# Loading and converting the first layer's weights in units of one m instead of one k

## The chip, the cores and the metric

The kernel runs on one core of one Trainium2 chip. The metric is the device time of one execution in microseconds; a smaller number is better. Over three runs the kernel before has a median of 731.37 us (729.12 to 733.59).

## The reference, cut to what matters

```python
def reference(**kw):
    y = rwkv(r, k, v, w, u)            # (4, 8, 768, 48): a state per head, decayed by w per token
    x = y.transpose(0, 2, 1, 3).reshape(3072, 384)
    h = np.maximum(x @ w_in, 0.0)      # w_in  (384, 2048)
    x = h * h @ w_out                  # w_out (2048, 384)
    h = x @ w2_in                      # w2_in (384, 1024)
    sm = softmax(h)
    ln = layer_norm(h * sm) * g_ln
    return ln @ w2_out                 # w2_out (1024, 384)
```

All four weight matrices arrive as 8-byte floats, the rest as 4-byte floats. "First layer" below is the pair w_in and w_out.

## The kernel before, in words

Three stages follow one another on TensorE (PE): attention, first layer, second layer. Tokens go in 24 chunks of 128 (chunk c); four chunks make a block n of 512 tokens, and there are 6 blocks. Chunks 0 to 3 are block 0; the attention of chunks 4 to 7 (block 1) is interleaved with the first layer of block 0, and so on.

The first layer takes w_in's 2048 columns in 16 groups m of 128. A step is one (block, m); block 0's m = 0 to 3 are split in two steps of 256 tokens each, because chunks 0 and 1 are ready before 2 and 3. Each step has two parts. **P1** (`p1`, L650 to L659) is nine matmuls: for each k of 3, high x by high w_in, low x by high w_in, high x by low w_in. ScalarE (ACT) then applies relu and square and makes the high part `gh` (L656 to L658), and VectorE (DVE) the low part `gl` (L659). **P2** (`p2`, L669 to L673) is nine matmuls of gh and gl with w_out's 128 rows of this m, added up over m in three PSUM banks. P1 runs up to three steps ahead of P2.

Weights come as 8-byte floats and are turned into two 4-byte parts, high and low. A load puts one unit into one of six staging buffers `stg` (SyncE, SP, issues all loads in order). `w1_conv` converts a unit: DVE makes a 4-byte float in three operations (L591, L594, L597, with PSUM bank 2 as scratch), ACT casts the high part (L609, `wih` or `woh`), GpSimd (POOL) subtracts for the low part (L610, `wil` or `wol`), and the next load is issued for the freed buffer. A unit of w_in before is (k, g): 128 rows by 512 columns (512 KB), so that the four m of group g need three units. A unit of w_out is one m: 128 rows by 384 columns (384 KB).

What decides a chunk's x: its scores on PE (L424, later L437), a masked copy on DVE (L473, later L481, "the mask"), the product with v on PE (L540, later L514), and the split into `xh` on ACT (L570) and `xl` on DVE (L571). From chunk 4 on, ACT copies L514's result to `ys` and eight small DMAs (L524, L526) bring it to `xr` before the split. Chunk 7 is the last that block 1's first P1 needs.

A scheduler places the instructions of each engine when the kernel is built, by its own estimates; from then on every engine, and SP with its DMAs, runs strictly in that order. It starts from the order of the code, where `side[i]` is the list of extra work (conversions, attention) put ahead of step i.

Of the kernel before, what the change touches and what calls it, by code (L numbers as in the profile page):

```python
# [18 lines left out]
DM = H * D  # L19
KD = DM // 128  # L20
# [13 lines left out]
M1 = FF1 // 128  # L34
# [3 lines left out]
NST = 6  # L38
# [139 lines left out]
def rwkv_moe_moe2_kernel(ctx, tc, rkd, tok, tk2, wd, w, u, w_in, w_out, w2_in, w2_out, g_ln, out):  # L178
    nc = tc.nc
# [5 lines left out]
    ps = psp.tile([128, 8, 512], F32, name="ps")  # L185
# [62 lines left out]
            )  # L248

    def setup_masks():  # L250
        make_identity(nc, ident)
        nc.gpsimd.memset(mask, 1.0)
        nc.gpsimd.affine_select(
            out=mask, in_=mask, pattern=[[1, C]], compare_op=ALU.is_gt, fill=0.0, base=0, channel_multiplier=-1
        )
        nc.gpsimd.memset(epst[:, 0:1], -0.5)
# [345 lines left out]
    def split(st, hi, lo, scale=None):  # L602

        x = as_f32(st, ps[:, 2, :].bitcast(U32))
        if scale is not None:
            nc.gpsimd.tensor_tensor(out=x, in0=x, in1=scale.to_broadcast(list(x.shape)), op=ALU.mult)

        def finish():
            nc.scalar.copy(hi, x)  # L609
            nc.gpsimd.tensor_tensor(out=lo, in0=x, in1=hi.bitcast(F32), op=ALU.subtract)  # L610

        return finish

    W1 = []
    for g in range(4):
        W1 += [(0, (k, g)) for k in range(KD)] + [(1, 4 * g + q) for q in range(4)]
    w_ld, w_st = [0], []

    def w1_load(n=1):
        for _ in range(n):  # L620
            if w_ld[0] < len(W1):
                kind, g = W1[w_ld[0]]
                w_st.append((kind, g, load_unit((w_in, w_out)[kind], kind, g, nc.sync)))
                w_ld[0] += 1

    def w1_conv():
        kind, g, st = w_st.pop(0)
        weight_tiles(kind, g // 4 if kind else g[1])
        if kind:
            split(st, woh[g // 4][:, g % 4], wol[g // 4][:, g % 4])()  # L630
        else:
            split(st, wih[g[1]][:, g[0]], wil[g[1]][:, g[0]])()
        w1_load()

    steps = []
# [244 lines left out]

    nsteps = len(steps)
    side = {i: [] for i in range(first_full)}
    first_m = {m: i for i, (n, m, c0, sz) in reversed(list(enumerate(steps))) if n == 0}
    for g in range(4):
        for q, n in enumerate((2, 2, 3) if g < 3 else (1, 1, 1, 1)):
            side[first_m[4 * g + q]] += [w1_conv] * n
    for c in range(4):
        side[c].append(lambda c=c: (first_state(c), load_chunk(4 + c) if c < 2 else None))
    for q, c in enumerate(range(4, 8)):
# [151 lines left out]
```

## Time and profile before

| | us |
|---|---|
| median of three runs | 731.37 |
| the profiled execution | 732.05 |
| its span | 730.3 |
| PE busy in the span | 702.9 (96%) |
| DVE busy | 418.7 (57%) |
| ACT busy | 321.7 (44%) |
| POOL busy | 267.9 (37%) |

The profile comes from one execution, and its span is what the trace covers; 1.75 us of that execution lie outside it. A busy share is an average over the whole span. The first 130 us, in which attention and weights arrive, look quite unlike the rest, so they have to be read by stretches. The timeline gives, for each engine, the start and duration of an instruction, and in brackets how long the engine had been idle before it and what ended the wait.

### The profile page before, as it was taken

Reading aid. Unit: us, or ns where it says so; the run is one execution under the profiler, and the core shown is the slowest. Engines: PE = TensorE matmul, PEld = TensorE weight load, DVE = VectorE, ACT = ScalarE, POOL = GpSimd, SP = SyncE. Lnnn points to the kernel's source line nnn. Section 1 sums busy time; section 2 is a strip of 40 time slices with the busy share of each in tenths; the row PEclk is TensorE's granted clock in tenths of the full one; section 3 lists DMA queues with packets and bytes.
Section 4 is the critical chain, followed back from the end, with each engine's and each line's share of the span. In section 5 each row is a group of like instructions: output and inputs, shape, how many; then the busy total and the mean of one; then the engine's idle time right before and its main releaser. Section 6 shows DMA issues by size and latency. Waiting matters only on the chain.

```text
span 730.3 us, 13143 instructions
## 1 busy us (share of the span) xinstructions
PE 702.9 (96%) x5088; PEld 599.7 (82%) x5088; DVE 418.7 (57%) x752; ACT 321.7 (44%) x625; POOL 267.9 (37%) x297
## 2 busy tenths in 40 slices
PE   3799999999999999999999999999999999999996
PEld 3588768788888888888888888888899999999996
DVE  7799986444534334433333266614768767777671
ACT  1444645454554554555454455634433232322232
POOL 6969777444533333334222022802303030300000
PEclk9999999999999999999999999999999999999999
DMA  8956552222312222321161016221111100000001
GB/s 277 267 200 212 140 179 79 89 67 85 106 57 89 67 66 66 108 65 60 41 202 35 12 41 202 88 86 34 66 65 49 40 22 11 22 22 22 22 34 38
DMA packets 35113, 62.73 MB, mean 86 GB/s; under 512 B 7777, under 2 KB 17378, under 8 KB 35042
## 3 DMA queue, kind: packets, MB, share of 16 engines
q1 hardware_dynamic: 35042, 61.80, 27.2%
q8 instruction: 42, 0.69, 0.4%
q14 instruction: 29, 0.24, 0.1%
HBM read 48.41 MB, written 9.44 MB: 79 GB/s over the span
## 4 chain that ended last, share of the span: by engine, by line
PE 86%; DMA 7%; SPq 2%; POOL 2%; ACT 1%; issue 1%; DVE 0%; ACTq 0%; POOLq 0%; DVEq 0%
PE ps L651 9%; PE ps L653 8%; PE ps L652 8%; PE ps L670 8%; PE ps L669 8%; PE ps L673 8%; PE ps L819 5%; PE ps L818 5%; PE ps L821 5%; PE ps L755 5%; PE ps L757 5%; PE ps L756 5%; DMA stg<-in_w_out_dram 3%; PE ps L802 3%; PE ps L514 2%; PE ps L437 2%
## 5 line engine op out<-in xcount | busy, mean ns | idle before, releaser
L659 DVE TENSOR_TENSOR gl<-ps,gh 128x512 fp32r<-128x512 f32 (+1 forms) x100 | 66.7, 668 | 168.2 <-ACT gh L658 166.9
L651 PE MATMUL ps<-xh,wih 128*128 128x512 f32 (+1 forms) x300 | 117.5, 393 | 1.8 <-ACT xh L570 1.0
L653 PE MATMUL ps<-xh,wil 128*128 128x512 f32 (+1 forms) x300 | 115.2, 385 | 2.3 <-POOL wil L610 2.3
L669 PE MATMUL ps<-gh,woh 128*128 128x512 f32 (+1 forms) x300 | 113.3, 383 | 2.2 <-ACT gh L658 2.1
L652 PE MATMUL ps<-xl,wih 128*128 128x512 f32 (+1 forms) x300 | 115.0, 384 | 0.1
L670 PE MATMUL ps<-gh,wol 128*128 128x512 f32 (+1 forms) x300 | 113.3, 383 | 0.0
L656 ACT ACTIVATE ps<-ps 128x512 f32<-128x512 f32 (+1 forms) x100 | 56.3, 564 | 115.9 <-PE ps L653 115.4
L356 POOL TENSOR_TENSOR mv<-mv,pt 48x512 f32<-48x512 f32 x40 | 52.1, 1302 | 93.0 <-DMA mv<-in_rkd_dram 92.3
L673 PE MATMUL ps<-gl,woh 128*128 128x512 f32 (+1 forms) x300 | 83.3, 382 | 0.0
L653 PEld LDWEIGHTS ps<-xh,wil 128*128 128x128 f32 x300 | 56.7, 189 | 14.3 <-POOL wil L610 3.1
L651 PEld LDWEIGHTS ps<-xh,wih 128*128 128x128 f32 x300 | 56.4, 189 | 14.5 <-ACT xh L570 1.6
L669 PEld LDWEIGHTS ps<-gh,woh 128*128 128x128 f32 x300 | 56.0, 189 | 13.9 <-ACT gh L658 2.9
L652 PEld LDWEIGHTS ps<-xl,wih 128*128 128x128 f32 x300 | 56.8, 190 | 10.8 <-DVE xl L571 0.6
L818 PE MATMUL ps<-w2oh,lth 128*128 128x384 f32 x192 | 65.1, 339 | 0.2 <-ACT lth L811 0.2
L670 PEld LDWEIGHTS ps<-gh,wol 128*128 128x128 f32 x300 | 56.1, 189 | 11.2 <-issue 0.4
L819 PE MATMUL ps<-w2ol,lth 128*128 128x384 f32 x192 | 65.2, 339 | 0.0
L673 PEld LDWEIGHTS ps<-gl,woh 128*128 128x128 f32 x300 | 55.7, 189 | 10.9
L658 ACT CAST gh<-ps 128x512 fp32r<-128x512 f32 (+1 forms) x100 | 56.9, 571 | 2.8
L657 ACT ACTIVATE ps<-ps 128x512 f32<-128x512 f32 (+1 forms) x100 | 56.4, 566 | 2.8
L755 PE MATMUL ps<-w2ih,xh 128*128 128x512 f32 x144 | 57.4, 398 | 0.0
L827 ACT COPY ob<-ps 128x384 f32<-128x384 f32 x24 | 11.5, 480 | 102.9 <-issue 81.2
L756 PE MATMUL ps<-w2il,xh 128*128 128x512 f32 x144 | 56.8, 395 | 0.0
(120 smaller groups left out, 1232.8 us busy)
## 6 DMA issues: line engine op xcount, KB each, us to landing
stg<-in_w_in_dram SPq DMA_DIRECT2D x18, 512.0 KB, 6.9
stg<-in_w_out_dram SPq DMA_DIRECT2D x24, 384.0 KB, 6.0
tok<-in_tk_dram SPq DMA_DIRECT2D x20, 384.0 KB, 3.6
x2d<-stg SPq DMA_DIRECT2D x18, 256.0 KB, 2.5
x2r<-x2d SPq DMA_DIRECT2D x6, 768.0 KB, 4.9
out_dram<-ob SPq DMA_DIRECT2D x24, 192.0 KB, 1.9
kd<-in_rkd_dram SPq DMA_DIRECT2D x20, 224.0 KB, 3.5
mv<-in_rkd_dram SPq DMA_DIRECT2D x40, 96.0 KB, 2.3
```

The costliest lines, as they stand in the source:

```text
L651: nc.tensor.matmul(hp, wih[g][:, k, f], xh[:, k, cs], start=(k == 0), stop=False)
L652: nc.tensor.matmul(hp, wih[g][:, k, f], xl[:, k, cs], start=False, stop=False)
L653: nc.tensor.matmul(hp, wil[g][:, k, f], xh[:, k, cs], start=False, stop=(k == KD - 1))
L658: nc.scalar.copy(gh, hp)
L659: nc.vector.tensor_tensor(out=gl, in0=hp, in1=gh.bitcast(F32), op=ALU.subtract)
L669: nc.tensor.matmul(acc[e], woh[m // 4][:, m % 4, f], gh, start=start, stop=False)
L670: nc.tensor.matmul(acc[e], wol[m // 4][:, m % 4, f], gh, start=False, stop=False)
L673: nc.tensor.matmul(acc[e], woh[m // 4][:, m % 4, f], gl, start=False, stop=stop)
L755: nc.tensor.matmul(o, x2h[j][:, k, s], w2["ih"][:, k, fs], start=(k == 0), stop=False)
L756: nc.tensor.matmul(o, x2h[j][:, k, s], w2["il"][:, k, fs], start=False, stop=False)
L818: nc.tensor.matmul(o, hi[:, m], w2["oh"][:, m], start=(m == 0), stop=False)
L819: nc.tensor.matmul(o, hi[:, m], w2["ol"][m // 4][:, m % 4], start=False, stop=False)
```

## The change

Both weights of the first layer come in units of one m. A unit of w_in is now 128 columns over all 384 rows (`load_w1`): 384 KB in rows of 1 KB, three per partition, where it was 512 KB in rows of 4 KB. Units of w_out stay as they were. There are 32 units instead of 28, all of 384 columns per partition. The order is in(0), in(1), out(0), in(2), out(1), ... in(7), out(6), out(7), and the same again for m = 8 to 15, where before three units of w_in were followed by four of w_out, four times. `side` gets two conversions per step for steps 0 to 2 and 12 to 18, and one for steps 3 to 11; before, a group's conversions stood at three or four of its steps. One memset of a piece of PSUM bank 2 is added (before, the wider units wrote there).

```diff
     def setup_masks():
+        nc.vector.memset(ps[32:64, 2, DM:], 0.0)
...
     def split(st, hi, lo, scale=None):
 
         x = as_f32(st, ps[:, 2, :].bitcast(U32))
+        if len(hi.shape) == 3:
+            x = x.rearrange("p (k f) -> p k f", k=KD)
...
     W1 = []
-    for g in range(4):
-        W1 += [(0, (k, g)) for k in range(KD)] + [(1, 4 * g + q) for q in range(4)]
+    for g in range(2):
+        ms = range(g * (M1 // 2), (g + 1) * (M1 // 2))
+        W1 += [(0, ms[0])]
+        for m in ms:
+            W1 += ([(0, m + 1)] if m + 1 in ms else []) + [(1, m)]
     w_ld, w_st = [0], []
+
+    def load_w1(kind, m):
+        st = mp.tile([128, 512], w_in.dtype, tag="stg", bufs=NST, name="stg")[:, :DM]
+        if kind:
+            nc.sync.dma_start(out=st, in_=w_out[m * 128:(m + 1) * 128])
+        else:
+            nc.sync.dma_start(
+                out=st.rearrange("p (k f) -> p k f", k=KD),
+                in_=w_in.rearrange("(k p) f -> p k f", k=KD)[:, :, m * 128:(m + 1) * 128],
+            )
+        return st
...
     def w1_conv():
-        kind, g, st = w_st.pop(0)
-        weight_tiles(kind, g // 4 if kind else g[1])
+        kind, m, st = w_st.pop(0)
+        g, q = divmod(m, 4)
+        weight_tiles(kind, g)
         if kind:
-            split(st, woh[g // 4][:, g % 4], wol[g // 4][:, g % 4])()
+            split(st, woh[g][:, q], wol[g][:, q])()
         else:
-            split(st, wih[g[1]][:, g[0]], wil[g[1]][:, g[0]])()
+            f = slice(q * 128, (q + 1) * 128)
+            split(st, wih[g][:, :, f], wil[g][:, :, f])()
         w1_load()
...
-    first_m = {m: i for i, (n, m, c0, sz) in reversed(list(enumerate(steps))) if n == 0}
-    for g in range(4):
-        for q, n in enumerate((2, 2, 3) if g < 3 else (1, 1, 1, 1)):
-            side[first_m[4 * g + q]] += [w1_conv] * n
+    for i in range(first_full - 1):
+        side[i] += [w1_conv] * (1 if 2 < i < 12 else 2)
```

Line numbers in the changed kernel are higher by 1 from L251 on, by 3 in `split`, by 20 from `p1` on.

How the order of instructions moves is shown at three places. First DVE, where the first two chunks' `xl` is made and the first weights are converted. Before (L591, L594 and L597 are the three operations of a unit; these are units 3 and 4 by their width):

```order
L591 TENSOR_SCALAR ps<-stg 128x512
L594 SCALAR_TENSOR_TENSOR ps<-stg,ps 128x512
L597 SCALAR_TENSOR_TENSOR stg<-stg,ps 128x512
L571 TENSOR_TENSOR xl<-ps,xh 128x3x128 x2
L591 TENSOR_SCALAR ps<-stg 128x384
L594 SCALAR_TENSOR_TENSOR ps<-stg,ps 128x384
L597 SCALAR_TENSOR_TENSOR stg<-stg,ps 128x384
```

The same place in the changed kernel, where the first two operations are the end of out(0) and the next unit is in(2):

```order
L595 SCALAR_TENSOR_TENSOR ps<-stg,ps 128x384
L598 SCALAR_TENSOR_TENSOR stg<-stg,ps 128x384
L572 TENSOR_TENSOR xl<-ps,xh 128x3x128
L592 TENSOR_SCALAR ps<-stg 128x384
L595 SCALAR_TENSOR_TENSOR ps<-stg,ps 128x384
L572 TENSOR_TENSOR xl<-ps,xh 128x3x128
L598 SCALAR_TENSOR_TENSOR stg<-stg,ps 128x384
```

Two operations of unit in(2) have moved between the `xl` of chunk 0 and that of chunk 1.

Second POOL, around the weights of m = 12. Before, the group of m = 12 to 15 is tile wil_1129, in three units:

```order
L351 TENSOR_TENSOR kd_964<-kd_964,pt_80 112x512
L402 AFFINE_SELECT mv1_96<-b_1216 64x512 x2
L610 TENSOR_TENSOR wol_997<-stg_857,woh_996 128x384
L385 TENSOR_TENSOR tok2_1348<-tok2_1348,ub2_85 128x384
L610 TENSOR_TENSOR wil_1129<-stg_864,wih_1128 128x512
L386 TENSOR_TENSOR tok2_1348<-tok2_1348 128x384
L356 TENSOR_TENSOR mv1_96<-mv1_96,pt_80 48x512 x2
L610 TENSOR_TENSOR wil_1129<-stg_871,wih_1128 128x512
L610 TENSOR_TENSOR wil_1129<-stg_1003,wih_1128 128x512
```

In the changed kernel wil_866 belongs to m = 8 to 11 (here in(11)) and wil_1144 to m = 12 to 15 (here in(12) and in(13)); kd_972 is chunk 7's, tok2_1377 chunk 8's:

```order
L352 TENSOR_TENSOR kd_972<-kd_972,pt_80 112x512
L613 TENSOR_TENSOR wil_866<-stg_827,wih_865 128x3x128
L613 TENSOR_TENSOR wol_1005<-stg_872,woh_1004 128x384
L403 AFFINE_SELECT mv1_96<-b_1235 64x512 x2
L386 TENSOR_TENSOR tok2_1377<-tok2_1377,ub2_85 128x384
L613 TENSOR_TENSOR wil_1144<-stg_943,wih_1143 128x3x128
L387 TENSOR_TENSOR tok2_1377<-tok2_1377 128x384
L613 TENSOR_TENSOR wol_1005<-stg_1011,woh_1004 128x384
L357 TENSOR_TENSOR mv1_96<-mv1_96,pt_80 48x512 x2
L613 TENSOR_TENSOR wil_1144<-stg_1018,wih_1143 128x3x128
```

The low part of m = 12 is complete after one unit instead of three, and units for single m now stand behind attention work that waits for DMAs of its own.

Third PE, near the end of block 0, around chunk 7's L514. Before it stands inside the P1 of m = 15, with all of P2 of m = 13 still to come:

```order
L651 MATMUL ps<-xh,wih 128x512
L514 MATMUL ps<-mv_96,vs_98 48x64 x16
L652 MATMUL ps<-xl,wih 128x512
L653 MATMUL ps<-xh,wil 128x512
L669 MATMUL ps<-gh,woh 128x512
```

In the changed kernel (L689 and L690 are P2's first six, L693 its last three, L515 is the product with v):

```order
L673 MATMUL ps<-xh,wil 128x512
L689 MATMUL ps<-gh,woh 128x512
L690 MATMUL ps<-gh,wol 128x512
L689 MATMUL ps<-gh,woh 128x512
L690 MATMUL ps<-gh,wol 128x512
L689 MATMUL ps<-gh,woh 128x512
L690 MATMUL ps<-gh,wol 128x512
L515 MATMUL ps<-mv_96,vs_98 48x64 x16
L693 MATMUL ps<-gl,woh 128x512 x3
```

Chunk 7's product has moved back by eight matmuls (two of P1, six of P2). From there to the end of the program PE's order is the same in both kernels.

## Rows read from the trace of the kernel before

**Rows 1.** Waits of PE, whole span, one row: us in total, times, longest.

```profile
PE ps L653 <- POOL wil L610: 2.3, 3, 1.1
```

**Rows 2.** The same view from 135 us to the end; its only row.

```profile
PE ps L818 <- ACT lth L811: 0.2, 1, 0.2
```

**Rows 3.** Stretches: us, then PE, PEld, DVE, ACT, POOL busy (count), PEclk, DMA, GB/s.

```profile
30.00:40.00 10.00, 7.88 (x67) 7.20 (x67) 6.96 (x14) 3.59 (x9) 9.77 (x10) 0.88 0.89 291
...
60.00:80.00 20.00, 20.00 (x213) 16.44 (x213) 19.19 (x37) 10.98 (x22) 18.15 (x18) 1.00 0.57 182
...
100.00:120.00 20.00, 18.29 (x167) 13.98 (x167) 17.06 (x30) 12.84 (x26) 16.11 (x16) 0.91 0.46 137
```

**Rows 4.** Timeline of PE, 26 to 37 us: start, duration, instruction, wait before it.

```profile
26.47 0.50 PE L653 MATMUL ps<-xh,wil 128*128 128x256 f32 x2 [1.08 <-POOL wil L610]
...
36.10 1.16 PE L424 MATMUL ps<-rkw 48*128 48x128 f32 x8 [2.12 <-DVE atw L473]
```

**Rows 5.** Timeline of DVE: its first wait, chunk 1's xl, unit out(3).

```profile
2.46 0.47 DVE L279 TENSOR_SCALAR pwr<-wdt 112x4 f32<-112x4 f32 x1 [1.53 <-DMA wdt<-in_wd_dram]
...
22.84 0.56 DVE L571 TENSOR_TENSOR xl<-ps,xh 128x384 fp32r<-128x384 f32 x1 [0.65 <-ACT xh L570]
...
33.66 0.56 DVE L591 TENSOR_SCALAR ps<-stg 128x384 uint32<-128x384 uint32 x1 [2.69 <-DMA stg<-in_w_out_dram]
```

**Rows 6.** Groups by shape, 0 to 160 us: count, busy us, mean ns, idle before.

```profile
L591 DVE TENSOR_SCALAR ps<-stg 128x384 uint32<-128x384 uint32 x16 | 8.9, 557 | 3.5 <-DMA stg<-in_w_out_dram 3.2
...
L591 DVE TENSOR_SCALAR ps<-stg 128x512 uint32<-128x512 uint32 x12 | 8.3, 690 | 2.3 <-DMA stg<-in_w_in_dram 2.1
...
L610 POOL TENSOR_TENSOR wol<-stg,woh 128x384 fp32r<-128x384 f32 x16 | 17.0, 1070 | 3.8 <-ACT woh L609 3.5
```

**Rows 7.** DMA queue, 10 to 20 us: packets, MB, share of 16 engines.

```profile
q1 hardware_dynamic: 868, 3.29, 103.0%
```

**Rows 8.** The same from 24 to 27 us, with packets by size.

```profile
DMA packets 928, 0.75 MB, mean 250 GB/s; under 512 B 615, under 2 KB 701, under 8 KB 927
...
q1 hardware_dynamic: 927, 0.73, 106.9%
```

**Rows 9.** Timeline of PE at chunk 5's L514.

```profile
86.23 1.10 PE L514 MATMUL ps<-mv,vs 112*48 112x64 f32 x32 [0.98 <-DVE mv L481]
```

**Rows 10.** Timeline of PE, 103 to 110 us, P1 of m = 12 and 13.

```profile
103.39 0.50 PE L653 MATMUL ps<-xh,wil 128*128 128x512 f32 x1 [0.62 <-POOL wil L610]
104.34 0.50 PE L651 MATMUL ps<-xh,wih 128*128 128x512 f32 x1 [0.45 <-ACT wih L609]
...
105.71 0.60 PE L653 MATMUL ps<-xh,wil 128*128 128x512 f32 x1 [0.64 <-POOL wil L610]
...
106.54 0.63 PE L652 MATMUL ps<-xl,wih 128*128 128x512 f32 x1
106.97 0.63 PE L653 MATMUL ps<-xh,wil 128*128 128x512 f32 x1
...
109.70 0.40 PE L669 MATMUL ps<-gh,woh 128*128 128x512 f32 x1
109.93 0.39 PE L670 MATMUL ps<-gh,wol 128*128 128x512 f32 x1
```

**Rows 11.** Timeline of ACT at chunk 5's xh.

```profile
100.76 0.52 ACT L570 CAST xh<-xr 128x384 fp32r<-128x384 f32 x1 [5.89 <-DMA xr<-ys]
```

**Rows 12.** Timeline of POOL at chunk 8's tok.

```profile
95.59 1.01 POOL L385 TENSOR_TENSOR tok<-tok,ub 128x384 f32<-128x384 f32 x1 [1.47 <-DMA tok<-in_tk_dram]
```

**Rows 13.** Timeline of PE, 119 to 131 us, the end of block 0.

```profile
119.55 1.10 PE L514 MATMUL ps<-mv,vs 112*48 112x64 f32 x32
...
127.38 0.92 PE L464 MATMUL ps<-vs,ktg 64*48 64x48 f32 x32
...
130.22 0.73 PE L651 MATMUL ps<-xh,wih 128*128 128x512 f32 x2 [0.97 <-ACT xh L570]
```

**Rows 14.** Timeline of ACT at chunk 7's xh.

```profile
129.65 0.51 ACT L570 CAST xh<-xr 128x384 fp32r<-128x384 f32 x1 [1.49 <-DMA xr<-ys]
```

More of the change, by code (lines that the diff above doesn't have):

```diff
@@ L622, in w1_load @@
                 kind, g = W1[w_ld[0]]
-                w_st.append((kind, g, load_unit((w_in, w_out)[kind], kind, g, nc.sync)))
+                w_st.append((kind, g, load_w1(kind, g)))
                 w_ld[0] += 1
     def w1_conv():
-        kind, g, st = w_st.pop(0)
-        weight_tiles(kind, g // 4 if kind else g[1])
+        kind, m, st = w_st.pop(0)
+        g, q = divmod(m, 4)
+        weight_tiles(kind, g)
         if kind:
-            split(st, woh[g // 4][:, g % 4], wol[g // 4][:, g % 4])()
+            split(st, woh[g][:, q], wol[g][:, q])()
         else:
-            split(st, wih[g[1]][:, g[0]], wil[g[1]][:, g[0]])()
+            f = slice(q * 128, (q + 1) * 128)
+            split(st, wih[g][:, :, f], wil[g][:, :, f])()
         w1_load()
```

## The prediction

> **What bounds the kernel now.** I read the waits of PE first, for the whole span and then from 135 us on. After 135 us PE waits once, 0.2 us [rows 2]; from chunk 7's L514 on its order is the same in both kernels. So the change can only move the moment at which PE starts block 1's first P1, 130.22 us [rows 13]; all behind it, 600 us, shifts as it stands. The question is what is late before that moment, and I read it by stretches.
>
> Between 60 and 80 us PE is busy all of the time (20.00 of 20) while DVE has 0.8 us to spare and POOL 1.9; from 100 to 120 PE has 1.7 us of gaps, and its clock is granted at 0.91 [rows 3]. The gaps, in order of time: 1.08 us for the low part of group 0's third unit and 2.12 us for chunk 2's mask [rows 4]; 0.98 us for chunk 5's mask [rows 9]; 0.62, 0.45 and 0.64 us for the second and third unit of the group of m = 12 to 15 [rows 10]; and 0.97 us at the end for chunk 7's xh [rows 13]. The first and the fourth are of one kind: PE needs the weights of one m and waits for those of four [rows 1, 10]. The second is a DMA's: DVE stood 2.69 us before unit out(3), until 33.66 us, with the mask behind it [rows 5].
>
> **The change, part by part.** The numbers are differences of the 130.22 us; plus is later.
>
> *Conversion itself.* A DVE operation takes 0.690 us for 512 columns and 0.557 for 384 [rows 6]. With three per unit, 28 units cost 12 x 3 x 0.690 + 16 x 3 x 0.557 = 51.6 us, and 32 units 32 x 3 x 0.557 = 53.5: 1.9 us more on DVE. ACT and POOL pay about 1 us each, four more fixed shares. Strided writes of the high and low part I take at the price of contiguous ones: xl in three pieces of 128 takes 0.56 us, like 384 contiguous columns [rows 5, 6]. Only DVE, full from 60 to 80 us, could pass this on; that is a rival. The new memset stands ahead of DVE's first instruction, which waits 1.53 us for data [rows 5]: nothing; without that wait it would cost a few tenths.
>
> *Start, to 50 us: -0.9.* Chunk 1's xl now has two operations of in(2) ahead of it, 2 x 0.56 us, where it waited 0.65 for ACT anyway [rows 5]; the first P1 starts about half a microsecond later. But the wait of 1.08 behind it goes, since m = 1 needs only the second unit, whose low part comes earlier on POOL. PE then runs into new waits of about the old length (the low parts of m = 2 and 3 stand behind attention work on POOL), but all of them end before the one that counts, chunk 2's mask. This one still stands on DVE behind the seventh unit, now out(2). Its load comes one place earlier in SP's order, and 384 KB less are ahead of it (three of the first six units shrink from 512 to 384 KB): 0.39 MB at 3.29 MB per 10 us [rows 7] is 1.2 us, less 0.3 for shorter rows (below). So the mask, and PE's L424 at 36.10, come 0.9 earlier. From there both chains (mask, product, xl) are DVE's, with equal work in both orders. Ends: -1.7, if PE also keeps its clock, granted at 0.88 from 30 to 40 us [rows 3]; +2.0, if short rows are slow.
>
> *50 to 90 us: -1.0.* PE has no gap to 80 us that weights could fill. At 86.23 it waits 0.98 for chunk 5's mask [rows 9]. In the new order eleven more matmuls (P1 of m = 10 and two of P2, 11 x 0.23 = 2.5 us) stand ahead of that L514, and before that mask DVE converts 21 units of 384 columns instead of 11 and 9 of 512, 1.9 us less. The wait is covered. Ends: -1.0 and 0.
>
> *95 to 110 us: -1.7.* The three waits, 1.71 us, are for units two and three of a group whose first m PE wants; the third was cast behind ACT's wait of 5.89 us for chunk 5's xr [rows 10, 11]. In the new order in(12)'s cast stands well ahead of that wait. With the gaps, the half-speed stretch behind them goes: eight matmuls at a spacing of 0.43 us (106.54 to 106.97) instead of 0.23 (109.70 to 109.93) [rows 10], 1.6 us. Together 3.3. What is late next is POOL: in(12)'s subtraction stands behind chunk 8's tok, which waited for its DMA until 95.59 us and took 1.01 [rows 12]. With 1.07 of its own [rows 6], it ends near 97.7. PE stands before chunk 5's L514 and P1 of m = 10 at 86.23 - 0.98 - 0.9 = 84.35, and in the new order has 38 matmuls, that L514 (1.1 us) and chunk 6's first products (127.38 to 129.25 for chunk 8's [rows 13], 1.9) before it wants this low part: 84.35 + 38 x 0.23 + 3.0 = 96.1, a new wait of 1.6. Net -1.7. Ends: -3.3, if that tok's load lands sooner, and +2.6 (rival B).
>
> *End of block 0: +1.8.* From the start of chunk 7's L514 to block 1's P1 pass 10.67 us (119.55 to 130.22) [rows 13], paced by ACT's copy, eight DMAs issued one after the other and the xh cast at 129.65 [rows 14]; no weight takes part. Before, the rest of P1, all of P2 for m = 13 to 15 and chunk 8's first products covered all but 0.97 us. Now L514 stands eight matmuls later: 8 x 0.23 = 1.8 us less cover, so the wait becomes 2.8. Ends: +1.8; 0, if PE reaches L514 late for another reason anyway.
>
> *Sum:* -0.9 - 1.0 - 1.7 + 1.8 = -1.8 us: a span of 728.5 instead of 730.3, and 730.25 for that execution, which at 732.05 lay 0.7 above the median. On the median of 731.37 this is **729.6 us**.
>
> **Rivals.**
>
> *A, the full gain.* Chunk 8's tok lands sooner, since in the new order fewer bytes of weights are queued ahead of it, and POOL follows. Then 3.3 instead of 1.7 is gained at 95 to 110 us: -0.9 - 1.0 - 3.3 + 1.8 = -3.4; with the clock kept at 36 us, -4.2. That is 727.2 to 728.0. For it: POOL is idle 3.9 of 20 us from 100 to 120 [rows 3]. Against it: DVE's spare time from 60 to 80 and 100 to 120 us is 0.8 and 2.9 us [rows 3], and 1.9 of it now goes to fixed shares, so that chunk 7's mask can hardly come more than 3 to 4 us sooner.
>
> *B, units just in time come late.* From m = 10 to 15 each low part stands on POOL behind some attention work that waits for its own DMA, and each P1 wants its unit within two steps. From in(12)'s low part to in(15)'s POOL has 15 operations of about 1.1 us [rows 6, 12], 16.5 us, and PE 55 matmuls and 3.0 us of attention, 15.6; with one more wait for a DMA of 1.5 us, as at 95.59, that is 2.4 us on top of the 1.6 at m = 12. With DVE's 1.9 and without the old 3.3 this is +2.6; with chunk 5's mask as late as before the -1.0 goes too, and the sum is -0.9 + 0 + 2.6 + 1.8 = +3.5: **734.9 us**, slower than before. It decides where a unit's low part ends later than PE's P1 of the m before. For it: DVE and POOL are nearly full from 60 to 80 us [rows 3], when m = 8 and 9 are converted. Against it: when PE wants m = 12, DVE has converted 24 units of 384 columns instead of 12 and 12 of 512, and from 100 to 120 us POOL is idle 3.9 of 20 us [rows 3].
>
> *C, chunk 7 is no sooner.* If the 1.9 us on DVE eat what is gained, chunk 7's mask and L514 stay at 119.55 whatever the gaps before; the gains are handed back as a wait there. The end is then at 0 to +0.8: 731.8 us.
>
> *D, short rows are slow.* From 10 to 20 us, 868 packets of 3.8 KB on average moved 3.29 MB at a share of 103% [rows 7]; from 24 to 27 us 927 packets of 0.8 KB moved 0.73 MB at 107% [rows 8]. Per MB this is 16 x 10 x 1.03 / 3.29 = 50 engine-us against 16 x 3 x 1.07 / 0.73 = 70. At that rate the 16 units of w_in (6.3 MB) take 7.9 us more of all 16 engines, and the four of the first 25 us 2.0: the start comes to +1.1 instead of -0.9, the sum to +0.2, 731.6 us. I take 0.3 in the sum and not 1.2, since 615 of the second stretch's 928 packets were under 512 bytes [rows 8]. The Trainium skill, DMA: Bandwidth & Descriptors, section Measured (under Bandwidth), advises batches of at least 1 MiB, and its section Anatomy of one DMA gives about 2.0 us plus the bytes over 436 GB/s for one load. By it, an estimate for 384 KB is 2.9 us and for 512 KB 3.2, so the weights one after the other would take 93 us instead of 85, 8 us more. This trace speaks against that rule here: loads overlap, and the stretch of rows 7 moved 329 GB/s with units of just these sizes.
>
> **How the numbers follow.** Chances: forecast 0.46, A 0.20, B 0.15, C 0.13, D 0.06. The range runs from 726.8 (A with the clock kept, 727.2, and a little spread) to 734.3, which leaves out the upper part of B and a little of A. A measurement of this kernel can tell about 0.5%, 3.7 us, from no change: below 727.7 or above 735.0. Faster takes half of A and a little of the forecast's own spread, 0.18; slower half of B and a little of C and D, 0.09; the rest, 0.73, is no difference.
>
> **What would show it.** Right: block 1's first P1 starts near 128.4 us, with a wait of 2 to 3 us for xh; no wait of L653 or L651 for wih or wil at m = 13 to 15, one under 2 us at m = 12; L424 after chunk 2's mask near 35.2; no wait of chunk 5's product. Wrong: a series of waits of P1 for wil from m = 10 on (B), a seventh unit landing later than 33.6 us (D), a wait for xh still near 1 us (then the last term was wrong), or PE waiting for anything at all after 135 us.

## The result and the profile after

The changed kernel is slower: a median of 735.38 us (734.75 to 736.47, six runs) against 731.06 (729.11 to 733.59, six runs), a ratio of 1.0072 (95%: 1.005 to 1.0093). The prediction was 729.6 us, within 726.8 to 734.3: wrong in its sign, and outside its range. The profiled execution of after took 734.75 us with a span of 733.0, 0.6 under its median, where that of before (732.05) lay 1.0 above this series' median; so the two traces differ by 2.7 us and the medians by 4.3.

Waits of PE in the changed kernel, from 60 to 140 us (us in total, times, longest); these are all:

```profile
PE ps L671 <- ACT xh L571: 3.8, 1, 3.8
PE ps L673 <- POOL wil L613: 1.0, 1, 1.0
PE ps L438 <- ACT ys L520: 0.6, 1, 0.6
PE ps L515 <- DVE mv L482: 0.3, 1, 0.3
```

The waits that the change was about have shrunk: of [rows 9, 10] the one for chunk 5's mask and those at m = 12 and 13 are gone, and one of 1.0 us at m = 15 is new. After 137 us PE waits 0.5 us in one place, as in [rows 2]. The single row that grew is the first: block 1's first P1 waits for chunk 7's xh, 0.97 us in [rows 13]. Timeline of PE at the end of block 0 (start, duration, instruction, wait before it):

```profile
118.72 1.10 PE L515 MATMUL ps<-mv,vs 112*48 112x64 f32 x32
...
124.73 0.92 PE L465 MATMUL ps<-vs,ktg 64*48 64x48 f32 x32
...
130.43 1.22 PE L671 MATMUL ps<-xh,wih 128*128 128x512 f32 x2 [3.83 <-ACT xh L571]
...
137.51 0.40 PE L689 MATMUL ps<-gh,woh 128*128 128x512 f32 x1
```

The first matmul of P2 in block 1 in the trace of before:

```profile
134.79 0.50 PE L669 MATMUL ps<-gh,woh 128*128 128x512 f32 x1
```

PE reaches chunk 8's products (L465) at 124.73 us instead of 127.38, 2.65 sooner (3.6 were forecast). Then it stands 3.83 us, and starts block 1 at 130.43 instead of 130.22. And it starts slowly: from here to the first matmul of P2 pass 7.08 us, where before it was 4.57 (130.22 to 134.79). The two-microsecond slices say why (length, busy time and count of PE, PEld, DVE, ACT, POOL, then the granted clock, DMA share and GB/s):

```profile
128.00:130.00 2.00, 0.00 (x0) 0.00 (x0) 0.56 (x2) 0.14 (x1) 0.00 (x0) 0.94 0.06 14
130.00:132.00 2.00, 1.57 (x4) 1.30 (x5) 0.83 (x2) 0.38 (x1) 0.91 (x1) 0.50 0.73 259
132.00:134.00 2.00, 2.00 (x6) 1.54 (x5) 0.00 (x0) 0.00 (x0) 0.36 (x1) 0.50 0.99 318
134.00:136.00 2.00, 2.00 (x6) 1.62 (x5) 0.00 (x0) 0.87 (x2) 0.96 (x1) 0.50 0.73 223
136.00:138.00 2.00, 2.00 (x9) 1.55 (x9) 0.69 (x1) 1.18 (x3) 1.92 (x3) 0.85 0.00 2
```

While PE idles the granted clock falls to 0.50 (1.2 instead of 2.4 GHz), and six matmuls fit into 2 us where nine do behind it. The account of the two traces is then: 2.65 sooner at chunk 8's products, 2.86 more wait (3.83 - 0.97), 2.51 for the half clock (7.08 - 4.57): +2.7 us, the difference of the spans. From that first matmul of P2 to the end both traces take 595.5 us (730.3 - 134.79, 733.0 - 137.51), so nothing is lost or gained behind it.

**How much of it is the clock?** One trace can't say, since such half-speed stretches come and go between executions of one program. But for every timed run of the later series the span and the mean granted clock are given, and span x (1 - clock) is the clock that was missing, in us. Over 108 runs of the kernel before it is 4.7 us on average, and a run with 1 us more of it is 0.95 us longer (correlation 0.70). So a difference between kernels can be split into missing clock and the rest. Over all 12 runs of the changed kernel, its second series below included (the clock of the runs of before beside the first series isn't on record), the missing clock is 6.1 us, 1.4 more than before (standard error about 0.3), and the rest 2.7 us more (0.3). **Two thirds of the loss are time in which PE does nothing or is late, one third is clock.** (The clock is printed to 0.001, 0.7 us of a single run, so only means are used.)

### The profile page after: what moved, and what is told of

It reads as the page before. It is cut to its first block, busy times and chain, and to the rows that moved or that the text cites. A ratio compares the mean times of both kernels' runs of the same rounds, so it can differ in the third digit from the quotient of the medians.

```text
span 733.0 us, 13184 instructions
## 1 busy us (share of the span) xinstructions
PE 702.3 (96%) x5088; PEld 600.4 (82%) x5088; DVE 414.8 (57%) x765; ACT 322.1 (44%) x629; POOL 269.3 (37%) x301
## 4 chain that ended last, share of the span: by engine, by line
PE 84%; DMA 4%; DVE 3%; issue 2%; POOL 2%; ACT 2%; SPq 2%; ACTq 0%; POOLq 0%; DVEq 0%
PE ps L671 9%; PE ps L673 8%; PE ps L672 8%; PE ps L689 8%; PE ps L690 8%; PE ps L693 8%; PE ps L839 4%; PE ps L775 4%; PE ps L838 4%; PE ps L776 4%; PE ps L777 4%; PE ps L841 4%; PE ps L822 3%; PE ps L515 2%; PE ps L438 2%
## 5 line engine op out<-in xcount | busy, mean ns | idle before, releaser
L689 PE MATMUL ps<-gh,woh 128*128 128x512 f32 (+1 forms) x300 | 113.4, 382 | 2.1 <-ACT woh L612 1.8
L690 PE MATMUL ps<-gh,wol 128*128 128x512 f32 (+1 forms) x300 | 113.0, 381 | 0.5 <-POOL wol L613 0.5
L357 POOL TENSOR_TENSOR mv<-mv,pt 48x512 f32<-48x512 f32 x40 | 52.4, 1310 | 95.6 <-DMA mv<-in_rkd_dram 94.9
L693 PE MATMUL ps<-gl,woh 128*128 128x512 f32 (+1 forms) x300 | 83.1, 381 | 0.0
L689 PEld LDWEIGHTS ps<-gh,woh 128*128 128x128 f32 x300 | 55.9, 188 | 13.4 <-ACT woh L612 2.0
L690 PEld LDWEIGHTS ps<-gh,wol 128*128 128x128 f32 x300 | 55.9, 188 | 11.6 <-POOL wol L613 0.7
L693 PEld LDWEIGHTS ps<-gl,woh 128*128 128x128 f32 x300 | 55.2, 188 | 10.9
```

The costliest lines, as they stand in the source:

```text
L689: nc.tensor.matmul(acc[e], woh[m // 4][:, m % 4, f], gh, start=start, stop=False)
L690: nc.tensor.matmul(acc[e], wol[m // 4][:, m % 4, f], gh, start=False, stop=False)
L693: nc.tensor.matmul(acc[e], woh[m // 4][:, m % 4, f], gl, start=False, stop=stop)
```

## The experiments

The table holds all runs of the series; the ratio is to the kernel before in the same series (18 to 35 runs of it, medians 730.4 to 731.7). "Clock" and "rest" are the differences of the mean to before in us, split as above, with standard errors of 0.4 to 0.9 each (1.05 for the clock of `oldorder`). "Wait" is PE's wait for chunk 7's xh at block 1's first P1 in the profiled execution.

| | median us | ratio (95%) | clock | rest | wait |
|---|---|---|---|---|---|
| after2 | 735.28 | 1.0051 (1.0035 to 1.0066) | +0.7 | +2.6 | 4.4 |
| no7 | 730.68 | 0.9978 (0.9958 to 0.9998) | +0.1 | -1.1 | none |
| no7_before | 730.70 | 0.9982 (0.9954 to 1.001) | 0.0 | 0.0 | none |
| fill | 735.20 | 1.0056 (1.0037 to 1.0076) | +0.5 | +4.4 | 0.6 |
| ysfirst | 734.91 | 1.0059 (1.0041 to 1.0077) | +1.1 | +3.1 | 1.6 |
| before_late | 732.43 | 1.0029 (1.0012 to 1.0047) | +0.5 | +1.6 | 1.9 |
| longrows | 734.47 | 1.0054 (1.0032 to 1.0077) | +2.6 | +1.5 | 4.1 |
| oldorder | 737.13 | 1.0072 (1.0056 to 1.0087) | +2.4 | +2.5 | 3.4 |
| oldlong | 734.76 | 1.0028 (0.9996 to 1.0059) | +0.3 | +2.0 | 2.6 |
| longys | 733.26 | 1.0034 (1.0012 to 1.0056) | +1.4 | +0.5 | 1.4 |
| start_after | 739.05 | 1.0086 (1.0051 to 1.012) | +6.2 | +1.0 | 1.6 |
| start_longys | 737.91 | 1.0083 (1.0057 to 1.011) | +5.6 | +0.8 | 1.3 |
| b10 | 734.17 | 1.0043 (1.0022 to 1.0064) | +1.0 | +2.0 | 1.7 |
| fix7 | 732.43 | 1.0023 (0.9999 to 1.0047) | -0.4 | +1.9 | none |
| fix7long | 732.51 | 1.0011 (0.9985 to 1.0036) | +0.1 | +0.8 | 1.6 |
| fix7_before | 731.10 | 0.999 (0.9962 to 1.0017) | +0.3 | -0.5 | 0.8 |

### Does the loss hang on chunk 7?

`after2` is the changed kernel again. 

> The changed kernel once more, unaltered, for a second profiled execution and a narrower interval on this chip. If the wait for xh and the half-speed stretch at the start of block 1 are the rule, they are here again (3 to 4 us of wait, first P1 to first L689 of that block near 7 us instead of 4.6); if they were one execution's chance, they are not. Time 735 us, ratio 1.006 to 1.007.

It repeats the loss, 1.0051, with the same row in its timeline:

```profile
131.54 0.99 PE L671 MATMUL ps<-xh,wih 128*128 128x512 f32 x2 [4.36 <-ACT xh L571]
```

`no7` and `no7_before` take the wait away: chunk 7's split reads chunk 6's data, in the changed kernel and in that before, so that nothing waits for chunk 7 and its own rows are left out of what follows.

```diff
-        xr = xr_t.pop(c)
+        xr = xr_t.pop(c) if c != 7 else keep[6]
+        keep[c] = xr
```

> The changed kernel, but chunk 7's xh and xl are made from chunk 6's xr, which is there earlier (so chunk 7's rows of the result are those of chunk 6; its scores, products and eight DMAs still run). Block 1's first P1 then waits for nothing of chunk 7. Theory C (what the change gains ahead of the boundary is handed back as the wait for chunk 7 and the half clock behind it): the wait of 3.8 to 4.4 us and 1.7 to 3.4 us of half clock go, 735.3 - 6 to 7 = 728.5 to 729.5 us, below the kernel before. Theory S (the late start and the units themselves cost PE's time): only part of it comes, 732 us or more.

> The kernel before with the same edit, chunk 7's split fed from chunk 6's xr. Its wait at the boundary is 0.97 us and there is no half clock behind it, so 731 - 1 = 730 us. Theory C: the changed kernel with this edit is 1 to 2 us faster than this one. Theory S: it is still 2 us or more slower than this one.

The two come out equal, 730.68 and 730.70 us. Waits of PE in `no7` from 60 to 140 us:

```profile
PE ps L675 <- POOL wil L615: 1.6, 1, 1.6
PE ps L438 <- ACT ys L520: 1.0, 1, 1.0
PE ps L515 <- DVE mv L482: 0.2, 1, 0.2
```

Without the wait for chunk 7 the change costs nothing: in this pair the whole loss hangs on it. It gains hardly anything either: the rest is 1.1 us less than in `no7_before`, with a standard error of 0.7. One limit of this pair: without the dependence the scheduler places the work around chunk 8 differently, so it takes away the wait and some of the order around it.

### The end of block 0: ACT's order, cover, half clock

In the changed kernel ACT copies chunk 7's product later. Timeline of ACT, after:

```profile
120.63 0.58 ACT L677 ACTIVATE ps<-ps 128x512 f32<-128x512 f32 x1
121.25 0.59 ACT L678 CAST gh<-ps 128x512 fp32r<-128x512 f32 x1
121.86 0.73 ACT L418 COPY vs<-sg 48x192 f32<-48x192 f32 x2
122.49 0.58 ACT L520 COPY ys<-ps 112x512 f32<-112x512 f32 x1
...
129.86 0.51 ACT L571 CAST xh<-xr 128x384 fp32r<-128x384 f32 x1 [2.33 <-DMA xr<-ys]
```

and before:

```profile
120.87 0.57 ACT L519 COPY ys<-ps 112x512 f32<-112x512 f32 x1
121.36 0.58 ACT L656 ACTIVATE ps<-ps 128x512 f32<-128x512 f32 x1
```

The copy starts 3.77 us after L515 (122.49 - 118.72) instead of 1.32 (120.87 - 119.55), because L515 moved back behind P1 of m = 15, whose relu, square and cast now stand ahead on ACT. From L515 to block 1's P1 pass 11.71 us instead of 10.67: of the 2.45 us by which the copy is later, 1.4 are made up behind it.

`ysfirst` puts the copy ahead again:

```diff
-        nc.scalar.activation(hp, hp, AF.Relu)
+        relu = nc.scalar.activation(hp, hp, AF.Relu)
+        if i == first_full - 1:
+            pin(relu)
```

> The changed kernel, with one order on ACT: chunk 7's copy to ys stands ahead of relu, square and cast of m = 15 (as in the kernel before), not behind them. Theory 1 (the new order on ACT made chunk 7's xh late, and the wait for it cost the clock): ys starts near 120.0 us instead of 122.49, xh ends near 128, block 1's first P1 starts 2.4 us sooner with a wait of about 1.4 us, and the half-speed stretch of 2.5 us goes: 735.4 - 4.9 = 730.5 us, ratio 0.999. Rival (the eight small DMAs or the loads in their queues set xh, not ys): xh stays near 130, 735 us.

```profile
130.47 0.73 PE L671 MATMUL ps<-xh,wih 128*128 128x512 f32 x2 [1.58 <-ACT xh L571]
```

The path is 10.71 us again and the wait 1.58, but P1 starts where it did, 130.47 (L515 came 1.0 us later in that execution), and the ratio is no smaller. Part of the gain is given back at once: with the copy ahead, PE waits 0.34 us for gh and 0.31 us for gl of m = 15, which it doesn't in the changed kernel. `before_late` does the opposite to the kernel before: chunk 7's copy and its DMAs behind the P1 three steps on. As built, two of chunk 9's loads also stand ahead of these DMAs on SP.

```diff
-        side[t + 2].append(lambda c=c: (pe_av(c, 0), load_chunk(c + 2)))
+        if c < 7:
+            side[t + 2].append(lambda c=c: (pe_av(c, 0)(), load_chunk(c + 2)))
+        else:
+            side[t + 2].append(lambda c=c: late.append((pe_av(c, 0), c)))
...
+        for f, c in late:
+            f()
+            load_chunk(c + 2)
```

> The kernel before with only the end of block 0 changed: chunk 7's copy to ys and its eight DMAs stand behind relu, square and cast of m = 15, as in the changed kernel; the weights come in the old units and order. Theory 1: ys about 2.3 us later, the wait for xh about 3.3 us instead of 0.97, and a half-speed stretch of about 2.5 us behind it: 731.1 + 2.3 + 2.5 = 735.9 us, ratio 1.0066. Rival a (a wait costs its own length only): 733.4 us. Rival b (the boundary is not what made the changed kernel slower): 731.1 us.

The path becomes 11.62 us and the wait 1.92, and the kernel's median is 2.0 us higher (1.0029). So a later copy alone costs about half of the loss where it is added; but moving it back alone, in an order where L515 itself has little cover, gave nothing. After its wait of 1.92 us the clock did not fall:

```profile
126.00:128.00 2.00, 1.09 (x4) 0.76 (x5) 1.69 (x4) 0.51 (x1) 0.00 (x0) 1.00 1.00 357
128.00:130.00 2.00, 2.00 (x10) 1.65 (x10) 0.00 (x0) 0.38 (x1) 0.22 (x1) 1.00 0.94 247
```

while it did after the 1.58 us in `ysfirst` (1.7 us of missing clock there). The length of the wait alone doesn't decide it.

`fill` keeps PE at work during the wait, with 16 matmuls whose result nobody reads:

```diff
+        if i == first_full:
+            for _ in range(16):
+                pin(nc.tensor.matmul(ps[:, 2, :], wih[0][:, 0, :128], xhl[0][0][:, 0, :], start=True, stop=True))
```

> The changed kernel with 16 extra matmuls (high w_in by the high x of block 0, into a part of PSUM that nobody reads then; their result is not used) between chunk 8's scores and block 1's first P1, where PE stood idle 3.83 us in the changed kernel. Theory 1 (the long wait itself costs TensorE's clock): block 1's first P1 starts at 130.4 us as before, but its matmuls come at a spacing of 0.23 us and not of 0.43 us for 13 of them; 2.5 us sooner, 732.9 us, a ratio of about 1.0025 to the kernel before. Rival (the half clock behind the wait has another cause, or the extra matmuls delay P1): the half-speed stretch stays, 735.4 us or more.

```profile
129.15 3.92 PE L952 MATMUL ps<-xh,wih 128*128 128x512 f32 x16
133.66 0.73 PE L671 MATMUL ps<-xh,wih 128*128 128x512 f32 x2 [0.58 <-ACT xh L571]
```

The clock stayed at 1.00 at the boundary, and P1 to the first P2 matmul took 4.60 us. Yet the median stayed (735.2), and the missing clock over its runs, +0.5 us, is that of `after2` within the error. The theory that the half clock behind the wait is the loss isn't borne out: it is dear in some executions, but the mean loses little by it. Why the rest is larger here (+4.4) stays open. In the one trace chunk 7 is late before the 16 matmuls begin: its mask starts at 119.56 us, 2.6 later than in after, and so does its product.

```profile
119.56 1.50 DVE L482 COPY_PREDICATED mv<-mask,ps 64x512 f32<-64x512 uint32 x2
121.34 0.88 PE L515 MATMUL ps<-mv,vs 112*48 112x64 f32 x24
```

So here P1 is late with its input, xh, for which it waits the last 0.58 us; whether the fillers hold it back in other executions no run shows.

### Short rows, the order of the units, the start

`longrows` lays w_in out by m in memory, so that a unit has rows of 3 KB; `oldorder` keeps the units of one m and their short rows, but loads and converts them in the old order (a group's four of w_in, then its four of w_out); `oldlong` is both; `longys` is `longrows` with `ysfirst`.

```diff
-            nc.sync.dma_start(
-                out=st.rearrange("p (k f) -> p k f", k=KD),
-                in_=w_in.rearrange("(k p) f -> p k f", k=KD)[:, :, m * 128:(m + 1) * 128],
-            )
+            nc.sync.dma_start(out=st, in_=w_inm[m * 128:(m + 1) * 128])
```

```diff
+    for g in range(4):
+        W1 += [(0, 4 * g + q) for q in range(4)] + [(1, 4 * g + q) for q in range(4)]
...
+        for q, n in enumerate((2, 2, 4) if g < 3 else (2, 1, 1, 1)):
+            side[first_m[4 * g + q]] += [w1_conv] * n
```

> The changed kernel with w_in laid out in memory so that a unit is 128 rows of 3 KB and not 384 pieces of 1 KB; sizes, order and every instruction are the same. Theory 1 (chunk 7's chain and the wait behind it set the end): the start may be up to 2 us sooner, but chunk 7's mask stays near 117 to 118.5 us and the boundary wait takes up the rest: 735.4 us, at best 734.5. Rival (the short rows' cost of the start carries to the end): 733.4 us or less, block 1's first P1 2 us sooner.

> The units of the changed kernel (one m each, 384 columns, 1 KB rows), but loaded and converted in the order of the kernel before: the four units of w_in of a group, then its four of w_out, with two, two and four conversions at a group's first three steps (the last group two and three times one). It does one part of the change alone: the size and form of the units without the new order. Theory O (the new order is what costs: it makes chunk 7's xh late): block 1's first P1 waits about 1 us, no half-speed stretch, 731 to 732 us, ratio 1.000 to 1.002. Theory U (the units themselves cost, by short rows at the start and 1.9 us more of DVE): first P1 near 24.4 us as in the changed kernel instead of 22.9, and 733.5 to 735.5 us, ratio 1.004 to 1.007.

> The same as the run with the new units in the old order, and w_in laid out in memory so that a unit is 128 rows of 3 KB instead of 384 pieces of 1 KB; every engine's order is the same as there. Theory R (short rows cost at the start and it carries to the end): 1.5 to 2 us less than the run with 1 KB rows. Rival (the end is set elsewhere): the same within 0.7 us.

> The changed kernel with both single mends together: rows of 3 KB for w_in, and chunk 7's copy to ys ahead of m = 15's relu on ACT. Each alone gave 0.5 to 1 us. Theory S (they work in series: the start brings chunk 7's chain forward, the order on ACT shortens its end, and the half clock behind the wait goes): 732 us, ratio 1.002. Rival (something else holds chunk 7, its loads or POOL): 734 to 735 us, ratio 1.005.

The first unit lands later in the trace of after. Timeline of DVE at the first conversion and chunk 1's scaling, after:

```profile
10.70 0.56 DVE L592 TENSOR_SCALAR ps<-stg 128x384 uint32<-128x384 uint32 x1 [2.84 <-DMA stg<-in_w_in_dram]
...
12.36 3.93 DVE L365 TENSOR_TENSOR mv<-mv,pt 112x256 f32<-112x256 f32 x4
```

and before, whose first unit has a third more bytes:

```profile
9.76 0.70 DVE L591 TENSOR_SCALAR ps<-stg 128x512 uint32<-128x512 uint32 x1 [1.89 <-DMA stg<-in_w_in_dram]
...
11.51 2.68 DVE L364 TENSOR_TENSOR mv<-mv,pt 112x256 f32<-112x256 f32 x4
```

In eight executions with rows of 1 KB, that of after and seven of the runs here, the first conversion starts at 10.62 to 11.45 us, in four with rows of 3 KB at 9.51 to 10.54. But in four with the old units and their rows of 4 KB it starts at 9.64 to 11.56, so executions of one order differ as much as the rows do. Over the whole kernel, rows of 3 KB bring 2.4 us in the old order (734.76 against 737.13 in one series), by the split nearly all of it clock, and nothing clear in the changed one (ratios of 1.0054 against 1.0072 and 1.0051). Both orders lose with units of one m; neither rows nor order alone is the cause. `oldlong` (1.0028, an interval that includes no difference) and `longys` (1.0034) lose about half as much as the changed kernel.

`start_after` brings chunk 1's loads ahead of the first unit of weights; `start_longys` is the same edit made to `longys`.

```diff
-    w1_load()
     load_chunk(1)
-    w1_load(2)
+    w1_load(3)
```

> The changed kernel with chunk 1's two loads issued ahead of the first unit of w_in (one place changed among the first loads), which also puts chunk 1's scaling on DVE ahead of that unit's conversion. Theory: DVE no longer waits for the first unit's landing (10.7 to 11.5 us) before it scales chunk 1, chunk 1's scores start near 12.5 us instead of 14.1 to 14.9, the first P1 near 23 instead of 24.4 to 25.2, and if the start carries to the end, 733.5 us. Rival (the end is set by chunk 7's chain, which does not start there): 735 us.

> The same place changed among the first loads, in the changed kernel with 3 KB rows and chunk 7's copy to ys first. Theory (three causes in series: short rows, the start, the end of block 0): 731 us, ratio 1.000. Rival: 733 us, as without the new order of loads.

The first P1 came at 22.87 and 21.58 us (24.42 in after, 22.86 before), and the two were the slowest kernels of all. PE then ran into its next wait for x, 4.03 us, and the clock fell behind it. `start_after`, timeline and slices:

```profile
27.41 0.58 PE L672 MATMUL ps<-xl,wih 128*128 128x256 f32 x1 [4.03 <-DVE xl L572]
```

```profile
28.00:30.00 2.00, 2.00 (x11) 2.00 (x11) 1.90 (x4) 0.86 (x3) 2.00 (x3) 0.50 0.74 164
30.00:32.00 2.00, 2.00 (x11) 2.00 (x11) 1.43 (x4) 1.43 (x5) 1.71 (x2) 0.50 0.79 245
```

Here the clock is the loss: 6.2 of 7.1 us, as means over all runs. A reading that no run tests: the work that PE has at the start is the same, so a sooner start leaves longer waits between its parts, and the clock falls behind them. That the changed kernel is slow for its later start isn't borne out: starting sooner made it slower.

### What holds chunk 7

Chunk 7's mask on DVE starts at 116.94 us in after and at 116.97 in before, although its scores on PE run 4 us earlier (108.67 instead of 112.61). So near a match is a chance of two executions: in the old order the mask starts at 115.75 in the trace of `fix7_before` and at 121.77 in that of `no7_before`, in the changed one at 117.51 in `after2` and at 119.56 in `fill`. Timeline of DVE, after:

```profile
114.56 0.55 DVE L398 TENSOR_REDUCE b<-tok 128x8 f32<-128x384 f32 x1 [3.39 <-POOL tok L387]
115.03 0.88 DVE L572 TENSOR_TENSOR xl<-xr,xh 128x384 fp32r<-128x384 f32 x1
...
116.94 1.51 DVE L482 COPY_PREDICATED mv<-mask,ps 64x512 f32<-64x512 uint32 x2
```

L398 is a reduction for chunk 10, three chunks ahead; DVE, in order, stands 3.39 us before it, with chunk 7's mask behind. It waits for POOL, which itself waited only 0.50 us for the load of that token; between its two operations on it POOL makes a unit's low part (L613) and scales a chunk (L357):

```profile
109.73 1.02 POOL L386 TENSOR_TENSOR tok<-tok,ub 128x384 f32<-128x384 f32 x1 [0.50 <-DMA tok<-in_tk_dram]
110.70 1.36 POOL L613 TENSOR_TENSOR wol<-stg,woh 128x384 fp32r<-128x384 f32 x1
112.14 1.30 POOL L357 TENSOR_TENSOR mv<-mv,pt 48x512 f32<-48x512 f32 x1
113.51 1.01 POOL L387 TENSOR_TENSOR tok<-tok 128x384 f32<-128x384 f32 x1
```

In before the same reduction stands ahead of chunk 7's mask too, but POOL's second operation starts at 109.83 us:

```profile
109.83 1.03 POOL L386 TENSOR_TENSOR tok<-tok 128x384 f32<-128x384 f32 x1
112.22 0.55 DVE L397 TENSOR_REDUCE b<-tok 128x8 f32<-128x384 f32 x1 [1.13 <-POOL mv L402]
```

What is new is POOL's order: the low part and the scaling have come ahead of L387, and the reduction starts 2.3 us later.

`b10` puts this reduction behind chunk 7's mask. `fix7` also puts P1 of m = 15 behind chunk 7's L515, so that it covers the path and its relu can't stand ahead of the copy; `fix7long` adds rows of 3 KB, and `fix7_before` makes the edits of `fix7` to the kernel before.

```diff
+        if c == 10:
+            behind(mask7[0])
...
+            mm = nc.tensor.matmul(hp, wih[g][:, k, f], xh[:, k, cs], start=(k == 0), stop=False)
+            if i == first_full - 1 and k == 0:
+                pin(mm)
```

> The changed kernel with one operation moved on DVE: chunk 10's reduction, which waits for chunk 10's tok, stands behind chunk 7's mask and not ahead of it. Theory M (that reduction holds the mask, but PE's order sets L515 only a few tenths later): the mask ends near 116.5 instead of 118.45 us, L515 comes two matmuls earlier in the new order, xh 0.5 us sooner, 734.8 us. Rival (the mask is all that holds chunk 7): 2 us less and the half clock too, 731 us.

> The same, and P1 of m = 15 kept behind chunk 7's L515 on PE: L515 then stands six matmuls earlier with six more behind it, and the copy to ys no longer stands behind m = 15's relu. Theory M: L515 at 117.3, block 1's first P1 at 127.8 us with a wait near 1 us and mostly no half clock behind it, 735.3 - 2.6 - 1.7 to 3.4 = 729.5 to 731 us. Rival (chunk 7 is held by its loads or by PE's own delays at the start): above 733 us.

> The same with w_in in rows of 3 KB. If the cost of short rows at the start (in(0) lands 0.9 us later with rows of 1 KB than with 3 KB) comes through once chunk 7 is free: 1 us less than the run before, 729 us, and faster than the kernel before. If something else is late then: the same as the run before.

> The two edits of order at chunk 7 in the kernel before. It waits 0.97 us for xh there and has no half clock behind it, so at most 1 us is to be had: 730 to 731 us. If the changed kernel with both edits is not faster than this one, the new units gain nothing of their own even with chunk 7 freed.

`b10`, timeline of DVE:

```profile
114.87 0.56 DVE L586 TENSOR_TENSOR xl<-xr,xh 128x384 fp32r<-128x384 f32 x1 [2.15 <-ACT xh L585]
...
116.43 1.49 DVE L494 COPY_PREDICATED mv<-mask,ps 64x512 f32<-64x512 uint32 x2
117.95 0.55 DVE L398 TENSOR_REDUCE b<-tok 128x8 f32<-128x384 f32 x1
```

The mask comes only 0.5 us sooner: with the reduction gone, DVE stands 2.15 us for chunk 6's xh, the end of the same kind of path one chunk earlier. `fix7` has no wait for xh at the boundary at all, only 0.53 for xl:

```profile
133.27 0.51 PE L688 MATMUL ps<-xl,wih 128*128 128x512 f32 x1 [0.53 <-DVE xl L586]
```

Its median is 732.43, and `fix7long`'s 732.51; both intervals include no difference from before. Against the changed kernel's 1.0072 and 1.0051 that gives back 2 to 3.5 us. The same edits in the kernel before bring 731.1, no change. By the means, 1.5 us of the 4.1 are left in `fix7`: none of the clock, but 1.9 (0.5) of the rest. So about two thirds of the loss go when chunk 7 is given cover; what the remaining 2 us of rest are, where `no7` has none, stays open. No version with the new units that does all of the work beats the kernel before.

## Why the prediction was wrong, point by point

| term | forecast | found |
|---|---|---|
| start, to 50 us | -0.9 | 0 |
| 50 to 90 us | -1.0 | about 0 |
| 95 to 110 us | -1.7 | -2.65 in the trace, 1.6 of it the clock of one execution |
| end of block 0 | +1.8 | +5.4 in the trace; about +3 without the clock |

**End of block 0: the step that failed.** "Now L514 stands eight matmuls later ... so the wait becomes 2.8." The cover behind it did shrink by 1.8 us, from 9.70 to 7.88. But the path was taken at its old 10.67 us, and ACT's order made it 11.71: of the moved L514 I counted the matmuls, and not what had moved ahead of its copy on ACT. With these two the wait is 0.97 + 1.82 + 1.04 = 3.83. The half clock behind it, 2.51 us in this trace, stood in no term.

**Chunk 7 is no sooner.** The forecast let L514 come earlier by all that PE gained before; L515 came at 118.72 instead of 119.55, 0.8 us. PE waited only 0.3 for the mask, but in these two traces the mask is at its old time. That is rival C's mechanism, at chance 0.13, and at a price of 0 to +0.8 it was too cheap: PE's gains were handed back at chunk 7, and then eight matmuls of cover were lost as well. It named "the 1.9 us on DVE" as the cause; the trace shows a 3.39 us wait for chunk 10's token instead, and `b10` that without it the mask comes only 0.5 us sooner: behind it stood chunk 6's xh.

**Start: 0 instead of -0.9.** Chunk 2's mask does come sooner, by 0.5 us (34.85 instead of 35.33). But PE's L425 behind it starts at 36.12 us, in [rows 4] at 36.10: three matmuls of P2 stand ahead of it, and they now wait 1.75 us for ACT's cast of woh. That wait stood in no term. The mask in before, and in after the mask and PE:

```profile
35.33 1.34 DVE L473 COPY_PREDICATED atw<-mask,ps 128x512 f32<-128x512 uint32 x2
...
34.85 1.36 DVE L474 COPY_PREDICATED atw<-mask,ps 128x512 f32<-128x512 uint32 x2
...
35.57 0.62 PE L689 MATMUL ps<-gh,woh 128*128 128x256 f32 x3 [1.75 <-ACT woh L612]
36.12 1.04 PE L425 MATMUL ps<-rkw 48*128 48x128 f32 x7
```

Two further costs are in the trace. The first conversion starts 0.94 us later, where I took 0.3 for the short rows; by the spread shown above, part of this may be the execution. Rival D's sign did not come: the seventh unit's conversion starts at 32.99 us, not later than 33.6. The 8 us beside that rival go by a formula that the Trainium skill, DMA: Bandwidth & Descriptors, section Anatomy of one DMA, gives for DMAs issued by GpSimd; these loads are issued by SyncE, and no run here shows that price. And chunk 1's scaling takes 3.93 us instead of 2.68, which stood in no term. POOL works beside it for 3.57 of the 3.93 us, and in before for 1.77 of 2.68; one such product takes 0.41 us at the least and 1.31 at the most. In four other traces in which POOL works beside them for at most 0.8 us, the four products take 1.4 to 1.7 us. The Trainium skill, GPSIMD Engine Reference, section 1. Specifications, says that GpSimd's SBUF interfaces are shared with VectorE and that DVE instructions with two SBUF inputs contend for them; this trace agrees, with a factor of three for the slowest.

**50 to 90 us: about 0 instead of -1.0.** Chunk 5's mask no longer stops PE, as forecast. But L515 there starts at 88.68 instead of 86.23, 2.45 later, and the eleven matmuls now ahead of it account for just that (2.5): PE is no further on than before. A part went in gaps where [rows 3] had none (19.69 us busy of 20.00):

```profile
60.00:80.00 20.00, 19.69 (x213) 15.96 (x212) 19.08 (x40) 10.49 (x22) 17.71 (x20) 1.00 0.62 183
```

In 50 to 60 us PE is busy for 9.71 of 10.00 us, where before it had no gap. The last 0.4 us I can't place.

**95 to 110 us.** The three waits and the half-speed stretch of [rows 10] are gone, and the wait forecast at m = 12 (1.6) came at m = 15 (1.01). PE comes out 2.65 ahead at chunk 8's products, more than the 1.7 of this term. But this is a difference of two traces; as one of the kernels it was too much: in three other traces of the old order (`before_late`, `no7_before`, `fix7_before`) the clock doesn't fall there. 1.6 us of "gain" were a chance of one execution. The recorded text's "chunk 8's tok", in [rows 12], in rival A and in the order of POOL, is a wrong name, too: tokens are prepared three chunks ahead, and it is chunk 9's. By the same lead chunk 10's reduction stands ahead of chunk 7's mask, in both kernels.

**Signs named ahead.** No wait of chunk 5's product, no waits at m = 13 and 14: right. The one wait under 2 us came at m = 15, not at m = 12, where it was forecast. Block 1's first P1 near 128.4: 130.43. A wait of 2 to 3 us for xh: 3.8 and 4.4. L424 (now L425) near 35.2: 36.12. Rival B did not occur: no series of waits for wil arose. Its figure, 734.9 us, is near the measured time for other reasons. Rival A's condition came, the token of rows 12 without a wait and 2.6 us sooner, and 2.65 of its 3.3 us with it at chunk 8's products; but the gain was lost at chunk 7.

```profile
92.96 1.00 POOL L386 TENSOR_TENSOR tok<-tok,ub 128x384 f32<-128x384 f32 x1
```

The view that all behind 130 us shifts as it stands held, except for the clock of the first 7 us.

**What stays open.** How the loss divides among the order on ACT, the lost cover, the late mask and the clock; why `ysfirst` alone brought nothing, though it shortened the path by 1.0 us, while `before_late`, its reverse, cost 2.0; why `fill` has a larger rest, and why `fix7` keeps 2 us of it; and what decides that the clock falls after one wait and not after a longer one. The Trainium skill, TensorE: Matmul & The Clock Gate, section What's actually happening, speaks of the ramp at a kernel's start: it puts its penalty under 1% of a typical span and calls it variable between runs. What the runs of before miss over the whole span, not at the start alone, is of that size, 4.7 us of 731 on average (0.6%); but this is as large as the effect that was to be measured.

## What to carry to other kernels

When an instruction moves back on one engine, compare what stands ahead of its successors on every engine down the path (here the copy on ACT, behind the P1 that had moved ahead), not only how much cover it has left. A gain ahead of a join is worth what the slower branch allows: look for the last arrival there first, here chunk 7's mask, which stood behind a prefetch for chunk 10 on an in-order engine, and then for what would hold it next: with the prefetch moved, chunk 6's xh did. Count a half-clock stretch as a gain only if several executions show it.

## What the runs showed of the hardware

- The clock differs from execution to execution of one program: over 108 runs of the kernel before the missing clock ranges from 1.5 to 9.6 us (mean clocks of 0.998 to 0.987), and explains about half of the variance of its times.
- A wait of 1.58 us was followed by half clock, one of 1.92 was not.
- Starting PE sooner can cost time: with the first P1 1.6 us sooner than in after, `start_after` has 10.8 us of missing clock in the mean, where after has 6.1.
- Four products of 112x256 floats on DVE take 1.4 to 1.7 us with POOL mostly idle beside them (four traces) and 3.93 us with POOL at work for 3.57 of them (after).
- The same first load can land up to 1.9 us apart between executions: with the old units the first conversion starts at 9.64 to 11.56 us in four traces. Rows of 1 KB (10.62 to 11.45) and of 3 KB (9.51 to 10.54) don't differ by more than that.
